# Two layers of attention and MLP: six maxima per three steps, and reciprocals of the sums taken once per head row

## The chip, the cores and the metric

The kernel runs on one core of a Trainium2 chip. The core has TensorE (PE; its weight loads are listed as PEld), VectorE (DVE), ScalarE (ACT), GpSimd (POOL) and SyncE (SP), which issues most of the DMAs. The metric is the device time of one execution in microseconds (us). A measurement is the median of several runs; the profile is one more execution, taken with the hardware profiler.

## The reference

Two rounds of an attention block and an MLP block, all in float32, over S = 2048 rows of D = 512, with 32 heads of 16:

```python
x = x + _A_ref(_layernorm(x), A_wqkv, A_wo)      # attention
x = x + _B_ref(_layernorm(x), B_w1, B_b1, B_w2)  # Dense(1792) -> mish -> Dense
# (both lines twice)
scores = jnp.einsum("bhqd,bhkd->bhqk", q, k) * (Dh ** -0.5)
p = _softmax(scores, axis=-1)
o = jnp.einsum("bhqk,bhkd->bhqd", p, v)
```

The softmax subtracts each row's maximum before the exponential and divides by the row's sum.

## The kernel before

**The layout.** The 2048 queries are cut into four chunks of 512 (`CW`), the 2048 keys into 16 tiles of 128. The 32 heads form eight groups of four (`HG`). A *block* is one group with one query chunk (32 blocks a layer); a *step* is one block's key tile: four heads, 128 keys, 512 queries. A layer's attention loop, `run` (L362), has 32 x 16 = 512 steps.

**What a step's work is.** The items of the loop are written as letters in the string `CYCLE` (L38), three strings for three steps:

- P, `pair` (L305): the scores of two heads, two matmuls into the two-bank tile sp (L314), and one exponential of 128 x 1024 on ScalarE (L315).
- S, `single` (L317): the scores of a third head into the one-bank tile ss (L324), and an exponential of 128 x 512 (L325). Four P and four S make the twelve heads of three steps.
- v, `pv` (L327): three quarters of a step's product p x v (L340), as column tiles of 32 for the four heads, accumulated over a block in one bank. The value tile has 32 columns a head (`VW`): 16 of v and 16 of ones, so the sums of p come out beside the product, sixteen times alike. A block's last quarter ends a call of `pv`; the quarters left over come in the next call.
- M, `max_mm` (L240): half a step's scores once more, without the maxima rows: two matmuls with queries on the partitions into a two-bank tile pm (L260), and a `tensor_reduce` on VectorE that takes the row maximum over 512 keys of two heads (L264). 32 such halves make a block, 1024 a layer.

The maxima run ahead of the scores: 24 steps (`AHEAD`, 48 halves) are done before the loop. When a block's 32 halves are complete, `max_fold` (L273) folds them to 16 numbers a query row, and, some ticks later (`self.later`, counted down by `tick`, L191), `max_rows` (L278) transposes them on TensorE (L283) into the bank that S uses, copies them negated on ScalarE (L286), splits them into two parts on GpSimd (L287, L288), and writes them by eight small DMAs on SyncE into two rows of the query tile qs (L292). A score matmul then has the maximum subtracted already.

When a block is complete, `drain` copies its accumulator (pv) to the tile ot on ScalarE (L359) and writes it to the DRAM buffer oscr (L360).

**The PSUM banks.** In the loop: two tiles pm of two banks, one tile sp of two, one for ss (and the transpose), one for the accumulator.

**The finish of a query chunk.** `heads_out(l, c, src)` (L464) reads chunk c from oscr: numerators and the sixteenfold sums as two tiles of 128 x 2048 (nd), by eight DMAs each on SyncE; takes the reciprocal of the sums (L473), the product (L474), and splits it into a rounded part oh on ScalarE (L477) and a rest ol on VectorE (L478). `wo_parts` (L481) then multiplies by the output weights and adds into x. The finishes of chunks 0 and 1 are hooked into the loop at steps 482 and 503; those of chunks 2 and 3 follow the loop. From step 488 on (`s + AHEAD >= STEPS`) one triple of chunk 0's wo matmuls is added in each step (`fill`).

**Who sets the order.** TensorE's order in the loop is fixed as written, by a chain of dependences (`pe`, L196). The other queues' orders come from a scheduler that lays the instructions out by an estimated timeline; each engine then runs its queue in order, and waits for what the head of its queue needs. Tiles of the pool `blk` (22 buffers: p, qs, ks, va, nd, oh, ol, weights) and of the tags raw, nm and others are given out in turn, so a new tile waits for the last use of an old one.

Of the kernel before, what the change touches and what calls it, by code (L numbers as in the profile page):

```python
# [9 lines left out]
F32 = mybir.dt.float32  # L10
# [3 lines left out]
ALU = mybir.AluOpType  # L14
# [4 lines left out]
P = 128  # L19
S, D, H, DH, F = 2048, 512, 32, 16, 1792  # L20
NCH = 4
CW = S // NCH
KT = D // P
# [4 lines left out]
VW = 32  # L28
# [6 lines left out]
HALF = 64  # L35
K_PARTS = (0, 0, 1)
Q_PARTS = (0, 1, 0)
CYCLE = ("PMvSM", "PvMSMPv", "MSMPvMS")  # L38
QW = CW // 4
AHEAD = 24  # L40
GSTEPS = NCH * NKT
STEPS = NG * GSTEPS
# [8 lines left out]
def kernel(ctx: ExitStack, tc: tile.TileContext, x, wqkv, wo, w1, b1, w2, out):  # L51
    nc = tc.nc
# [5 lines left out]
    tmp = ctx.enter_context(tc.tile_pool(name="tmp", bufs=2))  # L58
    ps = ctx.enter_context(tc.tile_pool(name="ps", bufs=2, space=PSUM))
    dram = ctx.enter_context(tc.tile_pool(name="dram", bufs=1, space=DRAM))  # L60
# [13 lines left out]
    def b8(shape, dt, name):  # L74
        return blk.tile(shape, dt, tag="blk", name=name)
# [3 lines left out]
    def open_banks():  # L79
        banks["pool"] = tc.tile_pool(name="sp", bufs=1, space=PSUM, reuse_waits="tile")  # L80
        banks["s"] = banks["pool"].__enter__()

    def close_banks():
        banks.pop("pool").__exit__(None, None, None)
        del banks["s"]
# [33 lines left out]
    def load_cols(w, j, name, **kw):  # L119
        return split_load(w[:, ts(j, 2 * P)].rearrange("(k p) n -> p k n", p=P), KT, 2 * P, name, **kw)  # L120

    def load_rows(w, j, name, **kw):
        return split_load(w[ts(j, 2 * P), :].rearrange("(k p) n -> p k n", p=P), 2, w.shape[1], name, **kw)
# [47 lines left out]
    def norm(src, nm, got, key, tag, fine=False):  # L171
        for _ in norm_parts(src, nm, got, key, tag, fine):
            pass
# [6 lines left out]
    class Attention:  # L180
# [92 lines left out]
        def max_fold(self, b):  # L273
            nm = tmp.tile([P, HG * NCH], F32, tag="nm", name=f"nm{self.l}{b}")
            nc.vector.tensor_reduce(nm, self.mxs.pop(b).rearrange("p h t a -> p (h t) a"), axis=AX.X, op=ALU.max)
            self.later.append((3, lambda: self.max_rows(b, nm)))

        def max_rows(self, b, nm):  # L278
            g, qb = divmod(b, NCH)
# [82 lines left out]
        def run(self, hooks, fill):  # L362
            self.prep_v(0)
            self.running = True
            close_banks()
            with tc.tile_pool(name="sa", bufs=1, space=PSUM, reuse_waits="tile") as self.pool:
                half, done = 2 * AHEAD, -4
                for s in range(STEPS + 4):
                    if s % GSTEPS == GSTEPS - NKT and s // GSTEPS + 1 < NG:
                        self.prep_v(s // GSTEPS + 1)  # L370
                    for item in CYCLE[s % 3]:
                        if item == "P":
                            self.pair()
                            self.drain()
                        elif item == "S":
                            self.single()
                        elif item == "M":
                            self.max_mm(half // 2, half % 2)
                            half += 1
                        else:  # L380
                            done += 1
                            self.pv(3 * done)
                    if s + AHEAD >= STEPS:
                        next(fill, None)
                    self.tick()
                    if s in hooks:
                        hooks[s]()
                self.drain()
                self.tick(99)
            open_banks()  # L390
# [71 lines left out]
        return att  # L462

    def heads_out(l, c, src):  # L464
        nd = []
        for a in range(2):
            t = b8([P, KT, CW], F32, f"nd{l}{c}{a}")
            for hh in range(P // DH):
                rows = src[c].rearrange("k g (h r) n -> k (g h) r n", r=VW)[:, hh, a * DH : (a + 1) * DH]
                nc.sync.dma_start(t[ts(hh, DH)], rows.rearrange("k d n -> d k n"))  # L470
            nd.append(t)
        num, den = nd
        nc.vector.reciprocal(den, den)  # L473
        nc.vector.tensor_tensor(num, num, den, op=ALU.mult)  # L474
        oh = b8([P, KT, CW], F32R, f"oh{l}{c}")
        ol = b8([P, KT, CW], F32R, f"ol{l}{c}")
        nc.scalar.activation(oh, num, AF.Copy)  # L477
        nc.vector.tensor_tensor(ol, num, oh.bitcast(F32), op=ALU.subtract)  # L478
        return oh, ol

    def wo_parts(l, c, outs, wot, x2, pe):  # L481
        oh, ol = outs[c]
        for t in range(NCH):
            if t % 2 == 0:
                acc = ps.tile([P, 2, 512], F32, tag="mx", name=f"wo{l}{c}{t}")
            for k in range(KT):
                mm3(
                    acc[:, t % 2],
                    [(oh[:, k, ts(t, P)], ol[:, k, ts(t, P)], wot[k // 2][:, 0, k % 2], wot[k // 2][:, 1, k % 2])],
                    first=k == 0,  # L490
                    last=k == KT - 1,
                    pe=pe,
                )
                yield
            if t % 2:
                x2v = x2[:, t - 1 : t + 1]
                nc.vector.tensor_tensor(x2v, acc, x2v, op=ALU.add)
# [85 lines left out]
    for l in range(2):  # L583
        if l == 0:
            order = [(0, 0), (4, 0), (0, 1), (4, 1), (1, 0), (0, 2), (4, 2), (1, 1), (0, 3), (4, 3)]
        else:
            order = [(0, 0), (0, 1), (0, 2), (4, 0), (4, 1), (4, 2), (1, 0), (0, 3), (4, 3)]
        order += [(m, c) for m in (1, 5, 2, 6, 3, 7) for c in range(NCH) if (m, c) not in order]
        att = qkv(l, wts, tt, order, late)
        wot, w1t, w2t, x2s, tts = [], [], [], [], {}  # L590
        xsrc = x if l == 0 else xs

        def load_res(c):
            x2 = b8([P, NCH, D], F32, f"x2{l}{c}")
            nc.sync.dma_start(x2, xsrc[ts(c, CW), :].rearrange("(t p) d -> p t d", p=P))
            x2s.append(x2)

        def load_w1(i, **kw):
            w1t.append(load_cols(w1, i, f"w1{l}{i}", **kw))

        def load_w2(i, **kw):
            w2t.append(load_rows(w2, i, f"w2{l}{i}", **kw))

        hooks = {}
        for i in range(2):
            hooks[STEPS - GSTEPS + 2 * i] = lambda i=i: wot.append(load_rows(wo, i, f"wo{l}{i}", hi="pool"))
            hooks[STEPS - 40 + i] = lambda i=i: load_res(i)
        hooks[STEPS - GSTEPS + 8] = lambda: load_w1(0, hi="pool")
        outs = {}

        def finish(c):
            outs[c] = heads_out(l, c, att.oscr)

        hooks[STEPS - 30] = lambda: finish(0)
        hooks[STEPS - 9] = lambda: finish(1)

        def wo_first():
            yield from wo_parts(l, 0, outs, wot, x2s[0], att.pe)

        fill = wo_first()  # L620
        att.run(hooks, fill)
        for c in range(NCH):
            if c + 2 < NCH:
                finish(c + 2)
            for _ in fill if c == 0 else wo_parts(l, c, outs, wot, x2s[c], lambda ins: ins):
                pass
            if c == 0:
                for i in range(1, 7):
                    load_w1(i, hi="dve")
                for i in range(4):  # L630
                    load_w2(i, hi="dve")
            if c + 2 < NCH:
                load_res(c + 2)
            if c == 1:
                norm(x2s[0], f"m{l}0", tts, 0, "acc")
                for i in range(4, 7):
                    load_w2(i, behind=True)
        hooks = {}
        for c in range(NCH - 1):
            spread(hooks, [(c, f) for f in range(5, 10)], x2s[c + 1], f"m{l}{c + 1}", tts, c + 1)  # L640
        wts, tt = {}, {}
        if l == 0:
            last = NCH - 1
            for f, js in ((2, (0,)), (4, (2,)), (9, (1,)), (11, (3,)), (12, (4,)), (13, (5,))):
                hooks.setdefault((last, f), []).append(lambda js=js: load_qkv(1, wts, js, behind=True, lo="dve"))
            for c in range(last):
                spread(hooks, [(last, f) for f in range(1 + 4 * c, 6 + 4 * c)], x2s[c], f"q1{c}", tt, c)
        mlp(l, x2s, w1t, w2t, tts, xs if l == 0 else out, hooks)
        if l == 0:
            late = lambda: norm(x2s[last], f"q1{last}", tt, last, "mx", True)  # L650
# [29 lines left out]
```

## Time and profile before

| | |
|---|---|
| time, median of 3 runs | 4218.78 us (4200.73 to 4254.07) |
| profiled execution: time, span | 4205.12 us, 4203.3 us |
| mean granted TensorE clock | 0.944 |
| attention loop of layer 1, first exponential to last drain | 199.2 to 1681.3 us |
| maxima of that loop: first, last | 199.4, 1381.9 us |
| attention loop of layer 2, last drain | 3769.9 us |
| reciprocals of the sums (L473) | 8, of 12.95 us |

The profile is that of one execution. Its page gives the busy time of each engine and the span in forty slices; other views give the same records as a timeline, by tile, or as sums in chosen windows. A row of a timeline reads: start, duration, engine, line, operation, output <- inputs, shapes, count, and in brackets the engine's idle time before it and what ended that. "PEclk", or the clock of a window, is the share of TensorE's full clock that was granted.

### The profile page before, as it was taken

How to read it: one execution, taken by the hardware profiler on the slowest of the kernel's cores; microseconds unless marked ns; L12 is line 12 of the kernel's file. 1: busy time of each engine (PE TensorE's matmuls, PEld its weight loads, DVE VectorE, ACT ScalarE, POOL GpSimd, SP SyncE). 2: the span in 40 equal slices, each digit the busy share in tenths (PEclk: the TensorE clock that was granted, in tenths of full speed). 3: DMA queues.
4: the chain of work that ended last, by engine and by line, in shares of the span. 5: the costliest groups of instructions: out<-in, count | busy, mean ns of one | idle time of the engine just before them, and what ended most of it. 6: DMA issues, size and time to landing. Idle time of an engine off the chain costs nothing. (4 is left out here: it accounts for less than half of the span.)

```text
span 4203.3 us, 69190 instructions
## 1 busy us (share of the span) xinstructions
PE 3801.0 (90%) x28784; PEld 2012.5 (48%) x28784; DVE 3083.0 (73%) x3000; ACT 2596.0 (62%) x3493; POOL 514.5 (12%) x443
## 2 busy tenths in 40 slices
PE   7999999999999977299989999999999999764999
PEld 5644444444444323277766444444444443233777
DVE  5679999999999112666656799999999991136655
ACT  2257777777777964044432577777777778641444
POOL 2100000000000100255420000000000001003545
PEclk9969999999999978699999699999999999886999
DMA  6511022022020122300055120221220201233000
GB/s 196 179 27 40 17 47 43 18 45 38 25 42 7 34 46 34 90 22 11 21 160 174 27 42 19 43 42 21 43 37 24 42 7 34 46 46 90 11 11 21
DMA packets 128298, 201.62 MB, mean 48 GB/s; under 512 B 16880, under 2 KB 65008, under 8 KB 121840
## 3 DMA queue, kind: packets, MB, share of 16 engines
q1 hardware_dynamic: 105744, 156.30, 16.5%
q10 hardware_dynamic: 22240, 40.90, 2.7%
q8 instruction: 226, 3.70, 0.4%
q14 instruction: 88, 0.72, 0.1%
HBM read 119.54 MB, written 75.50 MB: 46 GB/s over the span
## 5 line engine op out<-in xcount | busy, mean ns | idle before, releaser
L264 DVE TENSOR_REDUCE mxv<-pm 128x2 f32<-128x1024 f32 x2048 | 2360.7, 1217 | 195.6 <-PE pm L260 172.8
L315 ACT ACTIVATE p<-sp 128x1024 f32<-128x1024 f32 x1366 | 1397.9, 1023 | 180.2 <-PE sp L314 174.7
L340 PE MATMUL pv<-p,va 128*32 128x128 f32 (+3 forms) x16048 | 1204.2, 403 | 0.0
L260 PE MATMUL pm<-ks,qs 48*128 48x512 f32 x4096 | 1102.7, 489 | 73.2 <-DVE mxv L264 68.1
L325 ACT ACTIVATE p<-ss 128x512 f32<-128x512 f32 x1364 | 815.5, 598 | 482.2 <-PE ss L324 360.2
L314 PE MATMUL sp<-qs,ks 50*128 50x512 f32 x2732 | 707.0, 441 | 52.3 <-ACT p L315 50.6
L260 PEld LDWEIGHTS pm<-ks,qs 48*128 48x128 f32 x4096 | 427.3, 188 | 654.9 <-DVE mxv L264 526.9
L340 PEld LDWEIGHTS pv<-p,va 128*32 128x32 f32 x16048 | 376.1, 110 | 524.8 <-issue 457.7
L324 PE MATMUL ss<-qs,ks 50*128 50x512 f32 x1364 | 609.0, 446 | 0.0
L324 PEld LDWEIGHTS ss<-qs,ks 50*128 50x128 f32 x1364 | 260.2, 191 | 312.3 <-ACT p L325 203.6
L314 PEld LDWEIGHTS sp<-qs,ks 50*128 50x128 f32 x2732 | 304.2, 191 | 175.7 <-ACT p L315 145.4
L473 DVE RECIPROCAL nd<-nd 128x2048 f32<-128x2048 f32 x8 | 103.6, 12953 | 337.4 <-DMA nd<-oscr 185.7
L287 POOL CAST np<-nf 16x128 fp32r<-16x128 f32 x64 | 18.0, 281 | 2430.6 <-ACT nf L286 2358.0
L132 PE MATMUL wo<-wo,oh 128*128 128x512 f32 x128 | 60.9, 476 | 185.9 <-ACT oh L477 185.9
L522 DVE TENSOR_TENSOR al<-hb,ah 128x512 fp32r<-128x512 f32 x112 | 117.0, 1044 | 90.7 <-POOL hb L521 90.7
L518 POOL TENSOR_TENSOR hb<-hb,he 128x512 f32<-128x512 f32 x112 | 158.0, 1411 | 186.9 <-DVE he L515 174.6
L132 PE MATMUL h<-thm,w 128*128 128x512 f32 x448 | 177.1, 397 | 3.8 <-ACT thm L126 1.6
L521 POOL TENSOR_TENSOR hb<-hb,hr 128x512 f32<-128x512 f32 x112 | 162.5, 1451 | 136.9 <-DVE ah L520 114.6
L132 PE MATMUL mo<-w,ah 128*128 128x512 f32 x448 | 176.9, 395 | 1.6 <-DVE ah L520 1.5
L134 PE MATMUL mo<-w,al 128*128 128x512 f32 x448 | 161.9, 400 | 17.2 <-DVE al L522 17.0
L134 PE MATMUL h<-thm,w 128*128 128x512 f32 x448 | 176.3, 393 | 0.0
L133 PE MATMUL h<-tlm,w 128*128 128x512 f32 x448 | 176.2, 393 | 0.0
(162 smaller groups left out, 2858.8 us busy)
## 6 DMA issues: line engine op xcount, KB each, us to landing
scr<-pt ACTq DMA_DIRECT2D x64, 512.0 KB
qs<-scr SPq DMA_DIRECT2D x192, 128.0 KB
ks<-scr SPq DMA_DIRECT2D x192, 128.0 KB
vscr<-v SPq DMA_DIRECT2D x32, 512.0 KB
va<-vscr SPq DMA_DIRECT2D x64, 256.0 KB
oscr<-ot SPq DMA_DIRECT2D x64, 256.0 KB
nd<-oscr SPq DMA_DIRECT2D x128, 128.0 KB
qs<-np SPq DMA_DIRECT2D x512, 2.0 KB
```

What stands on the lines that cost most here:

```text
L132: pe(nc.tensor.matmul(acc, ah, bh, start=first and i == 0, stop=False))
L133: pe(nc.tensor.matmul(acc, ah, bl, start=False, stop=False))
L134: pe(nc.tensor.matmul(acc, al, bh, start=False, stop=last and i == n - 1))
L260: nc.tensor.matmul(pm[:, e], qs[u][rows, q0 : q0 + P], ks[u][rows, ts(n, 512)], start=True, stop=True)
L264: nc.vector.tensor_reduce(self.mxs[b][:, 2 * u : 2 * u + 2, qt, n], pm, axis=AX.X, op=ALU.max)
L314: self.pe(nc.tensor.matmul(sp[:, e], k, q, start=True, stop=True))
L315: nc.scalar.activation(self.pts[-1][:, 0:n], sp[:, 0:n], AF.Exp, scale=SCALE)
L324: self.pe(nc.tensor.matmul(sp, k, q, start=True, stop=True))
L325: nc.scalar.activation(self.pts[i // 3][:, 2], sp, AF.Exp, scale=SCALE)
L340: nc.tensor.matmul(self.accs[b][ts(h, VW), cols], self.va[b // NCH][:, kt, h, :], self.pts[j][:, e, cols], start=kt == 0 and q0 == 0, stop ...
L518: nc.gpsimd.tensor_tensor(hb, hb, e, op=ALU.mult)
L521: nc.gpsimd.tensor_tensor(hb, hb, r, op=ALU.mult)
```

## The change

In the loop, the cycle of items gets six M per three steps instead of seven. `tick` is called ahead of each v (four times per three steps) instead of once at the end of a step, and the row maxima's transpose falls due at the fourth tick instead of the third, so that it stands next to p x v. In the finish, one of the sixteen equal rows of sums is read for each of the 32 heads (den, 32 x 512), its reciprocal taken, written to a DRAM buffer (rscr) and read back sixteenfold into rec, a tile of 128 x 2048, by eight DMAs; these and the write are issued on GpSimd, the numerators' eight DMAs as before on SyncE. The finishes of chunks 0 and 1 are hooked in at steps 470 and 487.

```diff
-CYCLE = ("PMvSM", "PvMSMPv", "MSMPvMS")
+CYCLE = ("PMvSM", "PvMSPMv", "SMPvMS")
...
-            self.later.append((3, lambda: self.max_rows(b, nm)))
+            self.later.append((4, lambda: self.max_rows(b, nm)))
...
                         else:
+                            self.tick()
                             done += 1
                             self.pv(3 * done)
                     if s + AHEAD >= STEPS:
                         next(fill, None)
-                    self.tick()
...
     def heads_out(l, c, src):
-        nd = []
-        for a in range(2):
-            t = b8([P, KT, CW], F32, f"nd{l}{c}{a}")
-            for hh in range(P // DH):
-                rows = src[c].rearrange("k g (h r) n -> k (g h) r n", r=VW)[:, hh, a * DH : (a + 1) * DH]
-                nc.sync.dma_start(t[ts(hh, DH)], rows.rearrange("k d n -> d k n"))
-            nd.append(t)
-        num, den = nd
+        rows = src[c].rearrange("k g (h r) n -> k (g h) r n", r=VW)
+        num = b8([P, KT, CW], F32, f"num{l}{c}")
+        rec = b8([P, KT, CW], F32, f"rec{l}{c}")
+        den = tmp.tile([H, CW], F32, tag="raw", name=f"den{l}{c}", bufs=3)
+        rscr = dram.tile([KT, P // DH, CW], F32, name=f"rscr{l}{c}")
+        nc.sync.dma_start(den, src[c].rearrange("k g (h r) n -> (k g h) r n", r=VW)[:, DH])
         nc.vector.reciprocal(den, den)
-        nc.vector.tensor_tensor(num, num, den, op=ALU.mult)
+        nc.gpsimd.dma_start(rscr.rearrange("k h n -> (k h) n"), den)
+        for hh in range(P // DH):
+            nc.sync.dma_start(num[ts(hh, DH)], rows[:, hh, 0:DH].rearrange("k d n -> d k n"))
+        for hh in range(P // DH):
+            nc.gpsimd.dma_start(rec[ts(hh, DH)], rscr[:, hh][None].to_broadcast([DH, KT, CW]))
+        nc.vector.tensor_tensor(num, num, rec, op=ALU.mult)
...
-        hooks[STEPS - 30] = lambda: finish(0)
-        hooks[STEPS - 9] = lambda: finish(1)
+        hooks[STEPS - 42] = lambda: finish(0)
+        hooks[STEPS - 25] = lambda: finish(1)
```

## The prediction

> **What bounds the kernel now.** I read the page's busy times and slices first, then the timelines of VectorE, TensorE and ScalarE in one attention loop, then its end, last the windows with the granted clock.
>
> ```profile
> PE 3801.0 (90%) x28784; PEld 2012.5 (48%) x28784; DVE 3083.0 (73%) x3000; ACT 2596.0 (62%) x3493; POOL 514.5 (12%) x443
> PE   7999999999999977299989999999999999764999
> DVE  5679999999999112666656799999999991136655
> PEclk9969999999999978699999699999999999886999
> ```
>
> VectorE is full through most of each attention loop and then nearly idle for three slices: it ends its share early, while TensorE reads full throughout. So the loop has two stages, and a share over the whole span says little. In the first stage:
>
> ```profile
> 2699.36 20.85 DVE L264 TENSOR_REDUCE mxv<-pm 128x2 f32<-128x1024 f32 x18
> ```
>
> ```profile
> L315 ACT ACTIVATE p<-sp x387: 1017/1024/1043, 2499.5 to 3298.8; 128x1024 f32<-128x1024 f32 x194
> ```
>
> Eighteen maxima run with no gap, 20.85/18 = 1.158 us each. Three steps hold seven (8.11 us) and four exponentials of pairs; 386 intervals in 799.3 us make 2.071 a pair, 8.28 us per three steps. VectorE's maxima bound this stage, and 0.17 us per three steps is lost beside them. In the second stage no maxima are left:
>
> ```profile
> 3543.99 1.02 ACT L315 ACTIVATE p<-sp 128x1024 f32<-128x1024 f32 x1
> 3545.14 0.60 ACT L325 ACTIVATE p<-ss 128x512 f32<-128x512 f32 x1
> 3545.67 1.02 ACT L315 ACTIVATE p<-sp 128x1024 f32<-128x1024 f32 x1
> ```
>
> There ScalarE runs without a pause, 1.68 us from pair to pair, 6.72 per three steps.
>
> **Six maxima per three steps.** A loop of 512 steps has 1024 maxima, 48 of them done ahead. The 976 left last 418 steps at seven per three, and 488 at six. VectorE's total stays the same. What is won is that ScalarE's work of 70 more steps lies beside it, if TensorE keeps up:
>
> ```profile
> 2709.97 0.50 PE L324 MATMUL ss<-qs,ks 50*128 50x512 f32 x1
> 2709.97 0.73 PE L260 MATMUL pm<-ks,qs 48*128 48x512 f32 x2
> 2710.31 0.63 PE L314 MATMUL sp<-qs,ks 50*128 50x512 f32 x2
> 2710.87 0.86 PE L340 MATMUL pv<-p,va 128*32 128x128 f32 x16
> 2711.66 0.50 PE L260 MATMUL pm<-ks,qs 48*128 48x512 f32 x2
> 2712.00 0.39 PE L324 MATMUL ss<-qs,ks 50*128 50x512 f32 x1
> 2712.15 0.50 PE L260 MATMUL pm<-ks,qs 48*128 48x512 f32 x2
> 2712.49 0.40 PE L314 MATMUL sp<-qs,ks 50*128 50x512 f32 x2
> 2712.82 0.86 PE L340 MATMUL pv<-p,va 128*32 128x256 f32 x16
> 2713.61 0.49 PE L260 MATMUL pm<-ks,qs 48*128 48x512 f32 x2
> ```
>
> A group of single, maximum and pair takes 0.90 us (2709.97 to 2710.87), one with a second maximum 1.16 (2711.66 to 2712.82), p x v 0.79. The old cycle has one small group, three large and four p x v: 7.54 us, under the 8.11 of VectorE. The new one has two and two: 0.90 x 2 + 1.16 x 2 + 0.79 x 4 = 7.28. VectorE's is 6 x 1.158 = 6.95, ScalarE's 6.72. So TensorE becomes the bound, at 7.28 at least; with the same 0.17 lost beside it 7.45. Three engines within 8% of each other, each handing over through few PSUM banks, lose some more: I take 7.5, and 7.28 to 8.3 as ends (not above today's, since one maximum less cannot lengthen the cycle). 488 steps: 488/3 x 7.5 = 1220 us.
>
> The transpose of row maxima (L283), now ahead of p x v, has p x v to cover ScalarE's copy; its gain lies inside the 0.17. Its eight DMAs must land before the first scores of their block. A block's maxima now always end nine steps ahead, some 21 us; four ticks take 7.5, and then:
>
> ```profile
> 2655.84 0.28 PE L283 MATMUL nmt<-ident,nm 128*16 128x128 f32 x1
> ```
>
> ```profile
> 2656.85 5.07 SPq L292 DMA_DIRECT2D qs<-np  x8
> ```
>
> 6.1 us to the last issue, 3 more to land (below): 17. Cost nothing, with about 4 us of cover; gone, each us beyond it costs 32 us a layer.
>
> **The clock.** Columns: window, length, busy PE, PEld, DVE, ACT, POOL, clock.
>
> ```profile
> 215.00:230.00 15.00, 15.00 (x92) 6.96 (x85) 9.19 (x10) 6.65 (x9) 0.00 (x0) 0.50 0.00 1
> 290.00:305.00 15.00, 14.73 (x131) 6.45 (x130) 14.89 (x14) 11.52 (x16) 0.73 (x2) 1.00 0.09 13
> 1553.00:1581.00 28.00, 27.30 (x147) 10.35 (x147) 2.06 (x1) 14.48 (x19) 0.00 (x0) 0.50 0.00 1
> ```
>
> ```profile
> 217.69 1.02 ACT L315 ACTIVATE p<-sp 128x1024 f32<-128x1024 f32 x1 [0.31 <-PE sp L314]
> ...
> 230.98 1.02 ACT L315 ACTIVATE p<-sp 128x1024 f32<-128x1024 f32 x1 [0.26 <-PE sp L314]
> ```
>
> For about 85 us after the loop's start the clock is 0.50, TensorE is full, and three steps (four pairs) take 13.29 us. With six maxima I scale by 7.28/7.54: 12.8. The same 6.4 cycles then take 82 instead of 48 us: +34. [...]
>
> **The reciprocals in the loop.**
>
> ```profile
> 1550.83 1.91 ACT L477 ACTIVATE oh<-nd 128x2048 fp32r<-128x2048 f32 x1 [21.38 <-DVE nd L474]
> ```
>
> ```profile
> 1644.94 1.91 ACT L477 ACTIVATE oh<-nd 128x2048 fp32r<-128x2048 f32 x1 [22.64 <-DVE nd L474]
> ```
>
> Today ScalarE's queue holds the copy oh too early in both finishes, and the exponentials behind it wait 21.4 and 22.6 us; TensorE stops and its clock falls (window 1553:1581). The new chain from the drained accumulator: drain 0.6, a write to DRAM and the read of it, the reciprocal, a write, eight repeated reads on GpSimd's queue, the product. For a hop and for issues there are:
>
> ```profile
> 198.56 0.36 SPq L457 DMA_DIRECT2D vscr<-v  x1
> 201.54 0.33 SPq L235 DMA_DIRECT2D va<-vscr  x1
> ```
>
> ```profile
> 1682.34 3.24 SPq L470 DMA_DIRECT2D nd<-oscr  x7
> ```
>
> ```profile
> 1731.76 12.09 SPq L470 DMA_DIRECT2D nd<-oscr  x15
> ```
>
> ```profile
> 1691.01 12.95 DVE L473 RECIPROCAL nd<-nd 128x2048 f32<-128x2048 f32 x1 [6.38 <-DMA nd<-oscr]
> ```
>
> ```profile
> L474 DVE TENSOR_TENSOR nd<-nd,nd x8: 2291/2291/2292, 1548.5 to 3851.5; 128x2048 f32<-128x2048 f32 x8
> ```
>
> A hop is 3.0 us (201.54 - 198.56). The reciprocal takes 512 elements a partition instead of 2048: 12.95/4 = 3.24. Eight issues cost 0.46 to 0.81 each (3.24/7, 12.09/15): 3.7 to 6.4; no row shows GpSimd issuing a DMA, so these SyncE rows bound it. Landing after the last issue: 1691.01 - 1685.58 = 5.4. Sum: 0.6 + 3 x 3.0 + 3.24 + 3.7..6.4 + 5.4 + 2.29 = 24.2 to 26.9. In the changed kernel's order eleven exponentials (5.5 pairs, 10.3 us at 7.5 per cycle) stand on ScalarE between the drain and oh of the first finish, fifteen (14.1 us) in the second. So the stall is about 15 us and 11 us, not gone; it would be 0 if the chain were under 10. [...] Behind the first oh wait the exponentials; behind the product on VectorE wait block 31's maxima, and behind GpSimd's reads the split of block 30's row maxima, which has nine steps. VectorE's own added work amid maxima (3.24 + 2 x 2.29 + a wait on oh) mostly lies in that stall: +3. After it the clock falls as at 1553, and stays low until the first dense matmuls (wo, from step 488): up to 24 pairs at 3.2 instead of 1.88 us, 0 to 31; I take 18, as release within the stretch is possible.
>
> **The loop's end and after.**
>
> ```profile
> 1572.11 0.79 PE L132 MATMUL wo<-wo,oh 128*128 128x512 f32 x1
> ```
>
> ```profile
> 1681.33 0.60 ACT L359 ACTIVATE ot<-pv 128x512 f32<-128x512 f32 x1 [2.18 <-PE pv L340]
> ```
>
> ```profile
> 199.19 1.02 ACT L315 ACTIVATE p<-sp 128x1024 f32<-128x1024 f32 x1 [0.66 <-PE sp L314]
> ```
>
> ```profile
> 1790.42 0.65 DVE L513 TENSOR_SCALAR he<-hb 128x512 f32<-128x512 f32 x1 [5.23 <-ACT hb L512]
> ```
>
> From the first wo to the last drain 109.2 us, with the 22.6 stall; with 11 instead, 98. The new loop: 1220 + 34 + 3 + 15 + 18 + 98 = 1388, against 1681.3 - 199.2 = 1482: -94. After it, 109 us to the MLP. Finish 2's reciprocal (13 us) leaves the path, since its row can be done before the buffers of num and rec come free; finish 3 saves 9.7 and pays a hop of 3.0: -7. Together -20, between 0 (the reads on GpSimd wait behind its w1 and w2 splits) and -26. Per layer -114, two layers -228: from the profiled 4205 to 3977. That execution lay 0.3% under the median of the runs; I say 3980.
>
> **Rivals.** [...] (2) The cycle stays near today's 8.28 because of the shared banks, say 8.2: +0.7 x 162.7 = 114 a layer, 4205: no change. For it: three floors within 8%; against: the last stage shows ScalarE with TensorE handing over without loss. (3) Slower: the clock stays low in the loop. At the start it came back when this ran in one stretch:
>
> ```profile
> 281.27 2.36 PE L340 MATMUL pv<-p,va 128*32 128x512 f32 x16
> ```
>
> Five units of p x v at a block's edge; with three units an issue, such a run recurs only every 48 steps. Each step at low clock costs (12.8 - 7.5)/3 = 1.77 us. It is slower by 2% from (228 + 84)/1.77 = 176 more low steps; two missed edges in each layer are 192: 4317. For it: the first maxima stage is low for 85 us at full PE; against: the same edge released it in both layers.
>
> **The numbers.** Forecast 0.58 (own range 3900 to 4070), rival 1 0.22, rival 2 0.13, rival 3 0.07. The range 3840 to 4120 leaves out 2 in 10: rival 3, most of rival 2, the tail of rival 1. Two per cent, about what a measurement of this kernel can tell, is 4134 to 4303. Faster: forecast and rival 1, and a third of rival 2 in part: 0.86; same 0.09; slower 0.05.
>
> **What would show it.** Maxima spread to within 24 steps of the loop's end; pairs 7.3 to 7.7 us per four; VectorE no longer gapless; oh waits of some 15 and 11 us; reciprocals of 3.2 us; clock 0.50 after the first oh. Wrong if pairs stay at 8 or more per four, or if a wait on row maxima's DMAs stands before each block.

## The result, and the profile after

| | before | after |
|---|---|---|
| median | 4236.42 us (4 runs, 4200.73 to 4361.13) | 3990.76 us (4 runs, 3932.53 to 4041.99) |
| ratio of the runs within 1.5% of each kernel's fastest | | 0.932, 95% interval 0.917 to 0.946 |
| profiled execution | 4205.12 us | 4041.52 us |
| loop, first exponential to the end of the last drain, layers 1 and 2 | 1482.7, 1471.7 us | 1369.4, 1463.9 us |
| from there to the MLP, layers 1 and 2 | 108.5, 108.8 us | 87.6, 85.4 us |

The change is faster, by 5.8% between the medians and 6.8% between the runs within 1.5% of each kernel's fastest. The four runs after lie in two pairs, near 3936 and near 4042 us, and the profiled one is of the longer pair, at a mean clock of 0.911 against 0.938 and 0.939 in the shorter one. The shorter pair has no trace; where the longer one probably has its extra time is worked out below.

Of the page after, the busy times and three rows of slices:

```profile
PE 3807.9 (94%) x28784; PEld 2052.1 (51%) x28784; DVE 3059.7 (76%) x3000; ACT 2552.2 (63%) x3493; POOL 550.1 (14%) x515
PE   7999999999999897799899999999999999885999
DVE  5569999999999844566664558999999999525655
PEclk9969999999999858899997558999999999597999
```

VectorE's maxima now last to 1482.5 us in layer 1, 90 us before the loop's end (before: 1381.9, 300 us before it), and TensorE has gone from 90% to 94%. The row of the clock shows what is left: a slice at 0.5 at the end of each loop, and two at 0.5 at the start of the second one, where the page of before has one at 0.6.

The exponentials of pairs and the maxima in the middle of layer 1's loop, from the view of one tile and from VectorE's timeline:

```profile
L315 ACT ACTIVATE p<-sp x480: 1017/1024/1055, 419.4 to 1298.8; 128x1024 f32<-128x1024 f32 x160
```

```profile
899.73 10.69 DVE L264 TENSOR_REDUCE mxv<-pm 128x2 f32<-128x1024 f32 x9
910.75 10.68 DVE L264 TENSOR_REDUCE mxv<-pm 128x2 f32<-128x1024 f32 x9 [0.34 <-PE pm L260]
```

479 intervals in 879.4 us are 1.836 a pair, 7.34 us per three steps; by steps 96 to 416 it is 7.337 in layer 1 and 7.348 in layer 2. VectorE waits for TensorE's scores (0.34 us per nine maxima): TensorE is the bound.

The windows that matter, with the columns length, busy PE, PEld, DVE, ACT, POOL, granted clock, DMA share and GB/s:

```profile
206.00:284.00 78.00, 77.84 (x423) 33.51 (x425) 46.28 (x39) 39.48 (x52) 0.73 (x2) 0.50 0.18 33
1384.00:1486.00 102.00, 86.72 (x487) 36.91 (x487) 61.53 (x48) 43.27 (x55) 10.09 (x20) 0.51 0.34 65
2169.00:2452.00 283.00, 282.80 (x1555) 120.64 (x1553) 162.93 (x137) 140.45 (x184) 2.91 (x8) 0.50 0.10 21
2452.00:2470.00 18.00, 17.78 (x177) 8.25 (x173) 16.02 (x15) 14.41 (x20) 0.74 (x2) 1.00 0.24 35
```

The low clock after a loop's start lasts 78 us in layer 1 and 283 us in layer 2, with TensorE full in both. The second one ends here:

```profile
2242.52 2.36 PE L340 MATMUL pv<-p,va 128*32 128x512 f32 x16
2244.81 0.79 PE L324 MATMUL ss<-qs,ks 50*128 50x512 f32 x1
...
2449.97 2.20 PE L340 MATMUL pv<-p,va 128*32 128x512 f32 x16
2452.10 0.50 PE L324 MATMUL ss<-qs,ks 50*128 50x512 f32 x1
```

Both are runs of p x v five units long (a unit is a quarter of a step's product), at the end of the first block and of the fourth, 48 steps later. After the first a score still takes 0.79 us, after the second 0.50. In this trace and in that of before every record of the clock but the last lasts a whole multiple of 3.413 us (this stretch 283.31 us, 83 of them), so the clock changes on a grid. The stretch ended at 2451.9; counted back 61 times 3.413, a grid line stands at 2243.7, in the middle of the first run, while the second began inside a window (2448.5 to 2451.9) and had 1.9 us there. In layer 1 the run at 281.34 lay whole in the window that ended at 284.4, and the clock came back at the first block's end. The first 96 steps took 267.4 us in layer 1 and 356.6 in layer 2: 89 us, which is most of the 105 us between the two pairs of runs. That the shorter pair lacks this stretch is an inference from its mean clock: (1 - 0.939) / 0.5 of 3931 us is some 480 us at half clock, an estimate, against 723 in the trace, and layer 2's start has 205 us more than layer 1's.

And the first finish, on VectorE, TensorE and ScalarE:

```profile
1383.51 3.34 DVE L471 RECIPROCAL den<-den 32x512 f32<-32x512 f32 x1 [2.85 <-DMA den<-oscr]
1386.78 3.40 DVE L264 TENSOR_REDUCE mxv<-pm 128x2 f32<-128x1024 f32 x3
```

```profile
1387.98 0.80 PE L260 MATMUL pm<-ks,qs 48*128 48x512 f32 x2 [5.12 <-DVE mxv L264]
1411.50 0.80 PE L314 MATMUL sp<-qs,ks 50*128 50x512 f32 x2 [9.82 <-ACT p L315]
```

```profile
1408.63 1.91 ACT L480 ACTIVATE oh<-num 128x2048 fp32r<-128x2048 f32 x1 [9.75 <-DVE num L477]
```

The reciprocal stands at the head of VectorE's queue and waits 2.85 us for the sums, then takes 3.34. Behind it the maxima stop for 6.2 us; both pm tiles are full, and TensorE idles 5.12 us. The clock fell to 0.50 at 1386.9. That is 12 us before ScalarE's wait for oh's input begins (1408.63 - 9.75 = 1398.9) and 15 us before that wait stops TensorE (1411.50 - 9.82 = 1401.7); the clock stayed at 0.50 for 99 us.

### The profile page after: what moved, and what is told of

Same layout as the page of the kernel before. It is cut to its first block, busy times and chain, and to the rows that moved or that the text cites. A ratio compares the mean times of both kernels' runs of the same rounds, so it can differ in the third digit from the quotient of the medians.

```text
span 4039.7 us, 69275 instructions
## 1 busy us (share of the span) xinstructions
PE 3807.9 (94%) x28784; PEld 2052.1 (51%) x28784; DVE 3059.7 (76%) x3000; ACT 2552.2 (63%) x3493; POOL 550.1 (14%) x515
## 5 line engine op out<-in xcount | busy, mean ns | idle before, releaser
L264 DVE TENSOR_REDUCE mxv<-pm 128x2 f32<-128x1024 f32 x2048 | 2401.8, 1220 | 394.8 <-PE pm L260 345.4
L340 PE MATMUL pv<-p,va 128*32 128x128 f32 (+3 forms) x16048 | 1275.2, 423 | 0.0
L260 PE MATMUL pm<-ks,qs 48*128 48x512 f32 x4096 | 1222.0, 478 | 20.1 <-DVE mxv L264 18.0
L314 PE MATMUL sp<-qs,ks 50*128 50x512 f32 x2732 | 821.4, 471 | 34.0 <-ACT p L315 32.5
L260 PEld LDWEIGHTS pm<-ks,qs 48*128 48x128 f32 x4096 | 521.1, 199 | 430.9 <-DVE mxv L264 200.7
L340 PEld LDWEIGHTS pv<-p,va 128*32 128x32 f32 x16048 | 388.7, 114 | 559.4 <-issue 482.2
L324 PE MATMUL ss<-qs,ks 50*128 50x512 f32 x1364 | 654.5, 480 | 0.0
L314 PEld LDWEIGHTS sp<-qs,ks 50*128 50x128 f32 x2732 | 349.6, 201 | 229.8 <-ACT p L315 136.1
L132 PE MATMUL mo<-w,ah 128*128 128x512 f32 x448 | 176.4, 394 | 2.1 <-DVE ah L523 1.9
L133 PE MATMUL mo<-w,ah 128*128 128x512 f32 x448 | 175.1, 391 | 0.0
L519 ACT ACTIVATE hr<-he 128x512 f32<-128x512 f32 x112 | 70.9, 633 | 149.5 <-POOL hb L524 76.2
```

Source lines behind the costliest of these rows:

```text
L132: pe(nc.tensor.matmul(acc, ah, bh, start=first and i == 0, stop=False))
L133: pe(nc.tensor.matmul(acc, ah, bl, start=False, stop=False))
L260: nc.tensor.matmul(pm[:, e], qs[u][rows, q0 : q0 + P], ks[u][rows, ts(n, 512)], start=True, stop=True)
L264: nc.vector.tensor_reduce(self.mxs[b][:, 2 * u : 2 * u + 2, qt, n], pm, axis=AX.X, op=ALU.max)
L314: self.pe(nc.tensor.matmul(sp[:, e], k, q, start=True, stop=True))
L324: self.pe(nc.tensor.matmul(sp, k, q, start=True, stop=True))
```

## The experiments

Each is one kernel with the edit shown. Where one time is given, it is that of the profiled execution; where a kernel was timed in rounds, the median.

**1. The cycle alone.** The kernel before with the new `CYCLE`; `tick` and the finish as before.

```diff
-CYCLE = ("PMvSM", "PvMSMPv", "MSMPvMS")
+CYCLE = ("PMvSM", "PvMSPMv", "SMPvMS")
```

> Six maxima per three steps alone; ticks, finishes and their hooks as before. If the cycle carries the gain: three steps take 7.3 to 7.5 us at the full clock (8.28 before), the maxima end within 24 steps of the loop's end, and the time is near 4050 (about 85 us less a layer; the waits of oh stay at 20 us or more, and the 12.95 us reciprocal now stands among maxima). If the finish carries it: within 1% of before's run.

Measured: 4004.88 us (the kernel before on that chip: 4254.17); loops 1383.9 and 1368.2, after them 108.5 and 107.3, as before. The cycle is 7.42 us by steps 96 to 416, 7.43 by the row below (473 intervals in 878.6 us). It alone brings 99 and 103 us a layer.

```profile
L315 ACT ACTIVATE p<-sp x474: 1017/1023/1059, 419.6 to 1298.2; 128x1024 f32<-128x1024 f32 x158
```

**2. The finish alone.** The changed kernel with the old `CYCLE`, `tick` once a step and three ticks for the row maxima.

```diff
-CYCLE = ("PMvSM", "PvMSPMv", "SMPvMS")
+CYCLE = ("PMvSM", "PvMSMPv", "MSMPvMS")
```

> The new finish and its hooks alone; seven maxima per three steps and the tick as before. If the cycle carries the gain: three steps stay at 8.2 to 8.3 us, and only the finishes gain, the two waits of oh in a loop (44 us) falling to 25 or less and the time after the loop by some 15 to 20: near 4140. If the finish carries the gain: near 4000.

Measured: 4183.07 us. After the loops 84.1 and 85.4 us: the new finish is worth 24 us a layer there. In layer 1's loop it is worth 14 (1468.5 against 1482.7), with waits of oh of 18.3 and 14.4 us. Layer 2's loop took 1509.9, since the clock fell there in mid-loop, at 3108, for 119.5 us, the only mid-loop fall of that length in a trace. In the 3.4 us before it TensorE idled 1.0 us, 0.7 of it ahead of a transpose of row maxima; one stretch as idle in the same loops kept the full clock, so the cause is not shown.

**3. The old place of `tick`.** The changed kernel with `tick` at a step's end and three ticks.

```diff
-            self.later.append((4, lambda: self.max_rows(b, nm)))
+            self.later.append((3, lambda: self.max_rows(b, nm)))
...
-                            self.tick()
                             done += 1
...
+                    self.tick()
```

> The changed kernel with the row maxima's transpose back at the end of a step (third tick). If its place matters as the 0.17 us per three steps lost beside the maxima in before suggests: three steps at the full clock take 0.1 to 0.2 us longer on average than the changed kernel's 7.35, up to 30 us a layer. If it does not: the same 7.35.

The cycle is 7.417 and 7.422 us instead of 7.337 and 7.348. So the transpose's place next to p x v is worth 0.08 us per three steps, 13 us a layer. The time, 3963.48, says nothing of that, since the low clock at the loops' starts lasted 37.5 and 78.5 us here against 78.5 and 283.3.

Experiments 1 and 3 differ in the finish and its hooks alone. Behind its first 96 steps, a loop took 1114.0 and 1099.2 us with the old finish (layers 1 and 2 of experiment 1) and 1117.1 and 1115.9 with the new one. The stretch after the loop went from 108.5 and 107.3 to 85.4 and 85.6. So by these two traces the new finish, beside the new cycle, costs 3 and 17 us in the loop and gains 23 and 22 behind it; most of the change's gain is the cycle's. With the old cycle (experiment 2) the new finish gained in layer 1's loop too; there the maxima had ended before it.

**4. Dense runs of p x v.** The changed kernel with p x v in runs of six units, at every second v.

```diff
-                            self.pv(3 * done)
+                            if done % 2 == 0:
+                                self.pv(3 * done)
```

> The changed kernel with p x v issued in runs of six units every second time instead of three units each time. If an unbroken run of full-height matmuls in one stretch is what brings the clock back: the stretch at clock 0.50 after each loop's start lasts under 20 us in both layers (78 and 283 us in the changed kernel), and the one after the first finish ends early too. If the end of a block or the time since is what does it: 75 us or more again. The cycle itself should lengthen beyond 7.35 in both, since scores and maxima wait behind the longer run.

The low clock after a loop's start shrank to 10.2 us in both layers, and after the first finish to 34. But the cycle grew to 8.52 us, and the time was 4244.9. So here the clock returned sooner with the longer unbroken runs (10.2 us against 78.5 and 283.3), and with the spread ones the engines handed over better (7.34 us per three steps against 8.52).

**5. Dense matmuls at the start only.** The changed kernel with products of the identity by itself in the four v places at the loop's start where p x v has nothing to do.

```diff
+        def dense(self, n):
+            w = pbank("acc", f"dense{self.l}{self.dn}")
+            self.dn += 1
+            for _ in range(n):
+                self.pe(nc.tensor.matmul(w[:, 0:P], ident, ident, start=True, stop=True))
...
+                            if done <= 0:
+                                self.dense(24 if done == -3 else 3)
```

> The changed kernel with 33 extra 128x128x128 matmuls of the identity by itself, in the four places at the loop's start at which p x v has nothing to do yet (24 in the first, 3 in each of the others); they write a bank that p x v overwrites later, so nothing is computed otherwise. Theory: the clock stays at 0.50 after the loop's start only because TensorE then has narrow matmuls alone, and a dense full-height run brings it back or keeps it. Then the low stretch at the start (78.5 and 283 us in the changed kernel) shrinks to under 30 us in both layers, the first 48 steps of a layer take 117 to 130 us instead of 150 to 202, and the time is 3900 to 3960. Rival: the clock follows how full TensorE is over a longer time, whatever it runs; then the low stretches stay at 78 us or more and the time is 3990 to 4060. The stretch after the first finish is untouched by this: some 100 us in both theories.

3880.75 us, below the expected 3900. The same stretch of both layers, in windows:

```profile
202.00:284.00 82.00, 81.41 (x770) 41.69 (x768) 72.84 (x65) 64.43 (x87) 1.46 (x4) 1.00 0.30 54
2124.00:2206.00 82.00, 81.41 (x775) 41.47 (x777) 73.12 (x65) 64.47 (x88) 1.47 (x4) 1.00 0.28 52
```

The clock is 1.00 throughout, with TensorE busy for 81.41 of 82 us, about as full as in the window 206:284 of the changed kernel (77.84 of 78), where it was 0.50: what TensorE ran made the difference here, not how full it was. The first 96 steps take 240.3 and 240.2 us. At the first finishes the clock still fell (64.8 us low in three parts, and 99.0).

**6. The finish in three stages.** The loads two steps ahead of the reciprocal, the product and the copies 14 and 13 steps behind the loads.

```diff
+        yield
         nc.vector.reciprocal(den, den)
         nc.gpsimd.dma_start(rscr.rearrange("k h n -> (k h) n"), den)
...
+        yield
         nc.vector.tensor_tensor(num, num, rec, op=ALU.mult)
...
-        hooks[STEPS - 42] = lambda: finish(0)
-        hooks[STEPS - 25] = lambda: finish(1)
+        for c, at in ((0, (470, 472, 484)), (1, (487, 489, 500))):
+            stages = heads_out(l, c, att.oscr, outs)
+            for s in at:
+                hooks[s] = lambda old=hooks.get(s), stages=stages: (old and old(), next(stages))
```

> The changed kernel with each finish in the loop cut in three: the loads of sums and numerators at steps 470 and 487, the reciprocal with its write and repeated reads two steps later, the product and the split copies oh and ol at steps 484 and 500. Nothing is left out. Theory: the clock falls at the first finish because the reciprocal, at the head of VectorE's queue, waits 2.85 us for the sums and takes 3.34, so that the maxima stop and TensorE idles 5.1 us, and the wait of ScalarE for the product (9.75 us) prolongs it. With the reciprocal's data there before it comes up and the product late, TensorE idles under 4 us at the finish, the waits of oh are under 2 us, the low stretch near step 464 is under 40 us instead of 99 and 102, and the loop is 30 to 60 us shorter a layer: 3870 to 3960. Rival: the clock falls because of the 3.34 us reciprocal itself, or of transfers beside it, whatever waits there are; then the low stretch stays near 100 us and only the 12 us of oh's waits a layer go: 3950 to 4020.

Median 3953.41 us (3905.73 to 4013.28). The waits of oh are gone (0.0 in both finishes of both layers), yet the clock fell for 102.4 us in layer 1, and for 6.8 and 75.1 in layer 2: the expectation failed there, and oh's wait is not what drops the clock. The reciprocal still waited 2.97 and 3.36 us for the sums, since the order on VectorE comes from the scheduler's estimate of when data are there, not from the place in the program.

**7. The reads on SyncE.** The write of the reciprocals and the eight reads issued on SyncE instead of GpSimd.

```diff
-            nc.gpsimd.dma_start(rec[ts(hh, DH)], rscr[:, hh][None].to_broadcast([DH, KT, CW]))
+            nc.sync.dma_start(rec[ts(hh, DH)], rscr[:, hh][None].to_broadcast([DH, KT, CW]))
```

> The changed kernel with the write of the reciprocals and the eight repeated reads issued on SyncE instead of GpSimd; nothing is left out. Theory: GpSimd's queue costs the finish little inside the loop (its eight issues take 4.07 us and the reads land 3.6 to 11.1 us later, beside the loads of x that fill the DMA engines), so oh waits 8 to 11 us in the first finish as now (9.75); after the loop, where the write waits behind GpSimd's weight splits, the wait of the product (11.4 us in finish 3) falls by 3 to 7 us. Time within 15 us of the changed kernel's. Rival: the landing time is that of GpSimd's queue; then on SyncE the reads land within 4 us of the last issue, oh waits under 5 us in the first finish, and the time is 20 us or more shorter.

oh waited 7.7 and 7.8 us in the first finishes (9.75 and 9.71 before the edit), so the edit is worth some 2 us there. How much of that is GpSimd's queue is not shown: on SyncE the reads also kept back the loads of x, issued at 1398.56 instead of 1393.68. After the loop it went the other way than expected: oh of the third finish waited 11.7 us in both layers instead of 7.3 and 6.7, and the stretch after the loop grew to 92.3 and 88.6 us. The time, 3967.25, holds a start of 78.5 us in both layers.

**8. Stages and dense start together.**

> The finish cut in three together with the 33 extra matmuls at the loop's start, both as described for those two kernels alone; nothing is left out. Theory: the two gains add, since they lie at the two ends of a loop: low stretches under 30 us at the start and under 40 at the first finish, loops of 1320 to 1345 us, 3810 to 3890 in all, 0.90 to 0.92 of the kernel before. Rival: the clock's low share is made up elsewhere (a power budget that lasts): then low stretches appear in the middle of the loop and the time is 3930 or more.

Median 3852.11 us (3849.75 to 3854.37), 0.913 of the kernel before (0.909 to 0.918). Both gains are there (first 96 steps in 240.3 and 240.4 us, no wait of oh in the loop), no low stretch came up in mid-loop, and the runs now lie within 5 us of each other, against 109 us for the changed kernel. The sums were there in time now, and still:

```profile
1356.46 3.34 DVE L482 RECIPROCAL den<-den 32x512 f32<-32x512 f32 x1 [0.17 <-DMA den<-oscr]
```

```profile
1360.93 0.50 PE L260 MATMUL pm<-ks,qs 48*128 48x512 f32 x2 [2.98 <-DVE mxv L264]
1361.36 0.98 PE L340 MATMUL pv<-p,va 128*32 128x256 f32 x16
1362.27 0.79 PE L324 MATMUL ss<-qs,ks 50*128 50x512 f32 x1
```

Without any wait worth the name, the reciprocal's own 3.34 us empties TensorE for 2.98 us. The next matmul runs in 0.50 us, the one 1.3 us later in 0.79: the clock has fallen, and stays so for 82 us.

**9. A short reciprocal.** The changed kernel with the sums read as 128 x 128.

```diff
-        den = tmp.tile([H, CW], F32, tag="raw", name=f"den{l}{c}", bufs=3)
+        den = tmp.tile([P, H * CW // P], F32, tag="raw", name=f"den{l}{c}", bufs=3)
...
-        nc.sync.dma_start(den, src[c].rearrange("k g (h r) n -> (k g h) r n", r=VW)[:, DH])
+        nc.sync.dma_start(den, src[c].rearrange("k g (h r) (a b) -> (k g h) r a b", r=VW, b=P)[:, DH])
...
-        nc.gpsimd.dma_start(rscr.rearrange("k h n -> (k h) n"), den)
+        nc.gpsimd.dma_start(rscr.rearrange("k h (a b) -> (k h a) b", b=P), den)
```

> The changed kernel with one edit: the sums of a chunk are read as 128 x 128 instead of 32 x 512, so that the reciprocal takes a quarter of the elements a partition, about 0.85 us instead of 3.34; nothing is left out. Theory: any stop of the maxima of some 3 us empties TensorE and drops its clock; here the wait of VectorE for the sums (2.85 us before) and ScalarE's wait for the product (9.75) are still there, so the clock still falls at the first finish, near the reciprocal or at the wait of oh, and the low stretch is still some 70 to 110 us; oh's wait shrinks to about 7; the time falls by 10 to 30 us against runs of the changed kernel with the same start of the loop (3935). Rival: the length of the reciprocal alone decides; then the low stretch near step 464 is gone and each loop is 30 us or more shorter.

The reciprocal takes 0.95 us, but behind its wait of 3.29 TensorE idled 3.18 us, and the clock was low for one 3.4 us window. It fell for good 10 us later, when the product stood at VectorE's head and waited 9.96 us for the reads. oh waited 15.3 and 11.1 us, longer than expected, and the time was 4037.97, with a low start of 283 us in layer 2 like the changed kernel's. That is 4 us less than the changed kernel's profiled execution, one run each, and shows no gain.

**10. All three.** Number 8 with the short reciprocal.

> The kernel with the finish in three stages and the 33 extra matmuls, with the 128 x 128 reciprocal as well; nothing is left out. In that kernel without the short reciprocal TensorE idled 2.98 us behind the 3.34 us reciprocal and the clock fell 1.4 us later, for 82 and 99 us. Theory: with a reciprocal of 0.85 us, shorter than a maximum, TensorE does not idle there and the clock stays up until the product (2.28 us on VectorE) or the copy oh (1.91 us on ScalarE) at the earliest, 25 us later: low stretches at the finishes of 0 to 60 us, time 3780 to 3835. Rival: the transfers of the finish, or the wait for the sums, drop the clock: low stretch at the same place, 80 us or more, and the time stays at 3840 to 3860.

3815.27 us, within the expected range. Low clock in layer 1: 3.4 us behind the first product, then 30.7 behind the second finish's reciprocal, which waited 2.37 us for its sums; in layer 2: 51.2 behind the first product.

**11. Quarters.** Number 10 with the product, oh and ol in four quarters, at successive steps.

```diff
+        for k in range(KT + 2):
+            if k < KT:
+                nc.vector.tensor_tensor(num[:, k], num[:, k], rec[:, k], op=ALU.mult)
+            if 1 <= k <= KT:
+                nc.scalar.activation(oh[:, k - 1], num[:, k - 1], AF.Copy)
+            if k >= 2:
+                nc.vector.tensor_tensor(ol[:, k - 2], num[:, k - 2], oh[:, k - 2].bitcast(F32), op=ALU.subtract)
+            yield
```

> The kernel before this one with the product, oh and ol in four quarters (0.6 us each instead of 2.28, 1.91 and 2.29), one of each a step, from steps 484 and 500; nothing is left out. Theory: no single item on VectorE or ScalarE now stands longer than a maximum or an exponential, so the maxima and scores never stop and the clock stays up through both finishes in the loop: low stretches there under 25 us in all, s of 39 to 40 us per 16 steps up to step 480, loops of 1285 to 1310 us, 3750 to 3810 in all. Rival: the stretch does not depend on single items but on the finish as a whole; then it remains at 50 us or more and the time is that of the kernel with whole product, within 15 us.

Median 3816.9 us (3807.03 to 3820.24), no gain over number 10. VectorE's timeline shows why:

```profile
1379.21 2.50 DVE L492 TENSOR_TENSOR num<-num,rec 128x512 f32<-128x512 f32 x4 [1.11 <-DMA qs<-np]
...
1403.46 0.95 DVE L482 RECIPROCAL den<-den 128x128 f32<-128x128 f32 x1 [2.40 <-DMA den<-oscr]
```

```profile
1382.90 0.50 PE L260 MATMUL pm<-ks,qs 48*128 48x512 f32 x2 [3.13 <-DVE mxv L264]
...
1405.55 0.79 PE L260 MATMUL pm<-ks,qs 48*128 48x512 f32 x2 [2.81 <-DVE mxv L264]
```

The scheduler put the four quarters one behind the other, 2.50 us as before, so the edit did not do what it was for. The stops of 3.13 and 2.81 us are those two rows, and a low clock follows each.

**12. The order by hand.** Number 11 with dependences that fix places: the first reciprocal behind the maxima of step 474, the second reciprocal and both products behind the last maximum, each quarter of oh behind a step's exponentials; chunk 0's output weights begin eight steps later.

```diff
+    def behind(ins, prev):
+        if prev is not None:
+            tc.add_manual_dep(
+                ins.ins,
+                prev.ins.name,
+                mybir.DependencyInfo(mybir.DependencyClass.NoSync, mybir.DependencyReason.DATA),
+                reason="issue order",
+            )
...
-        nc.vector.reciprocal(den, den)
+        behind(nc.vector.reciprocal(den, den), att and att.mx)
```

> The kernel before this one with the order on VectorE and ScalarE fixed by hand: the reciprocal of the first finish stands behind 998 maxima (its sums should then be there), that of the second and both products behind the last maximum, the quarters of oh one behind each step's exponentials; the output weights of chunk 0 begin eight steps later. Nothing is left out. In the kernel before, the quarters of the product were put one behind the other on VectorE (2.50 us), TensorE idled 3.1 us there for one 3.4 us window of low clock, and 2.8 us behind the wait for the second finish's sums (2.4 us) and its reciprocal (0.95 us), for 31 and 51 us of low clock. Theory: with both gone from between the maxima TensorE has no idle stretch of 2 us or more before the last drain, no low clock stretch over 10 us in the loop, loops of 1270 to 1295 us, 3760 to 3800 in all. Rival: the work of the finish is as long wherever it stands and moves behind the loop: loops are 10 us or more shorter, but the stretch from the last drain to the MLP (80.8 and 79.2 us) grows by as much, and the time stays at 3805 to 3820.

Median 3763.53 us (3761.11 to 3765.95), 0.897 of the kernel before (0.894 to 0.900). VectorE around the reciprocal and the product, and the windows that stood at 0.50 and 0.51 in the changed kernel:

```profile
1371.30 1.23 DVE L264 TENSOR_REDUCE mxv<-pm 128x2 f32<-128x1024 f32 x1 [0.36 <-PE pm L260]
1372.44 0.94 DVE L491 RECIPROCAL den<-den 128x128 f32<-128x128 f32 x1
1373.30 14.01 DVE L264 TENSOR_REDUCE mxv<-pm 128x2 f32<-128x1024 f32 x12
1387.49 16.76 DVE L264 TENSOR_REDUCE mxv<-pm 128x2 f32<-128x1024 f32 x14 [0.17 <-PE pm L260]
1404.16 2.49 DVE L501 TENSOR_TENSOR num<-num,rec 128x512 f32<-128x512 f32 x4
```

```profile
203.00:284.00 81.00, 80.41 (x763) 41.11 (x764) 72.18 (x64) 63.83 (x86) 1.46 (x4) 1.00 0.30 54
1384.00:1486.00 102.00, 100.11 (x808) 46.44 (x806) 40.58 (x53) 72.08 (x98) 10.96 (x21) 1.00 0.36 66
```

One reciprocal of 0.94 us without a wait is all that stands between maxima; the product follows the last of them. No idle stretch of 1 us is left on TensorE in either loop, and no low window; the loops take 1278.9 and 1278.8 us. The rival had a share: the stretch after the loop grew from 80.8 and 79.2 to 86.8 and 87.2.

## Why the prediction came out as it did

**The bound and the cycle: right, a little too long.** It took 7.5 us where 7.28 was TensorE's floor; measured is 7.34, so the loss beside the floor is 0.06 and not 0.22. Over 488 steps that is 1194 us instead of 1220. Experiment 1 shows that the cycle carries most of the gain, and experiment 3 that the transpose's place gives 0.08 of it.

**The low clock after the loop's start: right in layer 1, not in layer 2.** The first 96 steps cost 267.4 - 32 x 7.34 = 32.5 us more than at full clock; the forecast was 34. In layer 2 they cost 356.6 - 32 x 7.35 = 121. The third rival's mechanism, a missed edge that recurs after 48 steps, happened once here: its price of 48 x 1.77 = 85 us stands beside the measured 89. The forecast had cases for no missed edge and for two in each layer, and none for a single one. Experiments 4 and 5 show what ends the stretch.

**The stalls of oh: the mechanism right, the size too large.** Forecast about 15 and 11 us; measured 9.75 and 2.42 in layer 1, 9.71 and 4.92 in layer 2. The chain was not shorter: the drain began at 1378.79 and oh at 1408.63, 29.8 us, against 24.2 to 26.9 forecast. The cover was longer: the eleven exponentials ahead of oh lasted from 1379.27 to 1398.89, 19.6 us instead of 10.3, since the stop of the maxima (5.82 us on ScalarE) and the low clock fell among them.

**The step that failed: the clock after the first finish.** The prediction let it fall behind oh's stall, priced it at 18 us, and put VectorE's own work at 3, since it "mostly lies in that stall". The profile shows the reverse order: the reciprocal at VectorE's head stops the maxima, TensorE idles 5.12 us, and the clock is low from there on for 99 us. First exponential to first output weight took 1283.5 us in layer 1; less 1194 and 32.5 that leaves 57 for the finish, where the forecast had 3 + 15 + 18 = 36. Experiment 6 shows that removing oh's wait leaves the low stretch, 8 that the reciprocal's length alone suffices, 10 and 11 that with a short one the fall moves to the next stop of the maxima, and 12 that with no such stop there is none.

**The rest.** First output weight to last drain: 86.0 us (98 forecast, as the second stall was shorter). After the loop: -21 and -23 us against -20, right; the third finish's wait of oh went from 24.5 to 7.3 and the fourth's from 56.7 to 51.3, near the -13 and -7 given. The row maxima's DMAs, put at nothing, cost nothing: no wait for them stands on TensorE between 290 and 1380 us.

**The sum.** Layer 1's loop came out at 1369.4 against 1388: -26 for the cycle, -1.5 for the start, +21 for the finish, -12 behind it. 3980 lies 11 us under the median. Part of that is luck: the median of two runs near 3936 and two near 4042 is the middle between them, where no run lies, and in layer 1 two errors met, a cycle priced too long and a finish priced too cheap. The profiled execution is 62 us above the forecast; without the 89 us of layer 2's start it would be 27 below. The low end of the range, 3840, for which rival 1 stands, leaves the stall of oh (15) and the low clock behind it (18) out of each layer and puts the cycle at 7.28; the trace of the changed kernel shows none of the three: in layer 1 oh waited 9.75 us, the clock was at 0.50 for 99 us, and the cycle took 7.34.

Left open: the falls in mid-loop in experiments 2 and 4; and the 39 us that TensorE still waits for oh of the last chunk in experiment 12, after the second loop, which were not worked on.

## What to carry to other kernels

When an engine becomes the bound, ask of every item queued on its feeders how long it holds them, wait included: here, in the changed kernel and experiments 4 to 11, the first idle stretch of TensorE over 2 us in a finish was 2.38 to 6.37 us long, and 3.4 to 120 us of half clock stood at or behind it. Move such items to where their feeder has no more work, and look at the order on the engine itself, since a place in the program need not be a place in its queue. Read the granted clock by stage before pricing anything at full speed; where runs of one kernel differ, the difference may sit in one stretch that can be removed.

## What the runs showed of the hardware

**Stops of 2.38 to 6.37 us had a low clock behind them.** In the traces of the changed kernel and of experiments 5 to 11, each layer's first idle stretch of TensorE over 2 us in the finish was 2.87 to 6.37 us long, and a low clock stood at or right behind it in all 16 cases. How long it lasted did not follow the stop: 3.4 us in four cases, 6.8 in one, 51 in two, 82 to 120 in nine. In experiment 4 first stops of 2.44 and 2.38 us had 34 us of low clock behind them, in experiment 6 a second one of 2.52 us had 75; idle stretches of 1.00 us in experiment 10 and 1.30 in experiment 8 had none. A stop is not the only way down: in mid-loop of experiment 4 the clock fell nine more times, for 3.4 or 6.8 us, behind grid windows (defined below) with 0.2 to 0.6 us of matmuls on 128 rows; other windows with as little kept it.

**The return went with full-height matmuls in one window.** In the traces of before, after and experiments 1, 3, 5 to 8, 10 and 11, I summed for each grid window (3.41 us from one grid line to the next) at low clock in which TensorE was busy for over 3.3 us the time of matmuls on 128 rows (all but the scores' with 48 and 50). Of 112 such windows that full clock followed, 101 had 2.0 us or more of them; of 609 that another low one followed, 36. Busy alone was not enough: TensorE was busy for 282.80 of 283.00 us of the changed kernel's longest stretch at 0.50, and in experiment 4 an idle stretch of 2.38 us, less than one window, had a low clock behind it. In the changed kernel a grid line cut the run of p x v at 2242.52, behind which the clock stayed at 0.50, and none the one at 281.34, behind which it was 1.00. Whether the place of such a run on the grid differs from one execution of a kernel to the next was not shown, as each kernel has one trace; if it does, it could explain that executions of the changed kernel differ by 109 us and those of the kernels with the dense start (experiments 8, 11 and 12) by 5 to 13.

**Reads that share the engines.** While the repeated reads landed in the changed kernel, the DMA engines were full:

```profile
1391.87 4.07 POOL L476 DMA_DIRECT2D rec<-rscr  x8 [4.00 <-PE ss L324]
```

```profile
1394.00:1408.00 14.00, 7.69 (x35) 2.89 (x31) 6.87 (x6) 2.22 (x3) 1.93 (x4) 0.50 1.00 211
```

GpSimd issues one in 0.51 us, within the bounds taken from SyncE; but the last read landed 10.3 us after the last issue ended (1395.94 to the product's start at 1406.25), at a DMA share of 1.00, with 2 MB of loads of x beside it. The prediction had 5.4. The write of the reciprocals took 3.1 us to land (median of eight), near the prediction's 3.0 for a hop.
